# Convolution steps spread evenly over the weight gradient phases, up to just ahead of the output phase

## The chip, the cores and the metric

One core of a Trainium2 chip runs the whole program. The metric is the time of one execution on the device in microseconds (us). The kernel before takes 2009.09 us, the median of three runs (2007.18 to 2009.27).

## The reference

The program is the forward and backward pass of a block that adds two branches: a long convolution (a shift filter of four taps, a product with v, a convolution of length 2048 by FFT, a gate), and a gated MLP. Cut to its core:

```python
def reference(A_q, A_k, A_v, A_shift_k, A_ssm_k, A_ssm_D, B_W_gate, B_W_up, B_W_down, B_x, grad_out):
    # x = A_q;  xn = layernorm(x)                      S, D, F = 2048, 1024, 3584
    # out = x + A(xn, k, v, shift_k, ssm_k, ssm_D) + B(xn, W_gate, W_up, W_down)
    # A: kv = shift(k) * v;  y = irfft(rfft(kv) * rfft(ssm_k)) + kv * D;  result xn * y
    # B: h = relu(xn W_gate) * (xn W_up);  result h W_down
    _out, _vjp = jax.vjp(_f, A_q, A_k, A_v, A_shift_k, A_ssm_k, A_ssm_D, B_W_gate, B_W_up, B_W_down)
    return (_out, *_vjp(grad_out))
```

## The kernel before

The MLP runs in phases: *hidden* (gate, up and their gradients), *down gradient* (`grad_down`), *input gradient* (`grad_in`, the gradients of the gate and up weights), then the *output phase* and the gradient of x. The first three are generators that yield after every eight matmuls of 512 columns, a slot with a declared length of 1730 ns. The convolution is a generator too, of 408 steps in eight groups of channels. A small loop weaves them: every slot pays its length times a *pace* into an account, and when the account is open, steps are taken and charged.

```python
    def mlp():
        yield 0.9, b.hidden(first, goT, B_W_gate, B_W_up, B_W_down, g, xn_d, h_d, ug_d)
        yield 1.3, b.grad_down(g, h_d, out_9)
        yield 1.3, b.grad_in(xn_d, ug_d, out_7, out_8)

    a_steps, left = a.steps(), A_START
    if True:
        for pace, phase in mlp():
            for ns in phase:
                left -= ns * pace
                while a_steps is not None and left <= 0:
                    d = next(a_steps, None)
                    if d is None:
                        a.close()
                        a_steps = None
                        b.open_right(B_W_down)
                    else:
                        left += d
```

When the convolution is done its buffers are released, and W_down is loaded in their place for the output phase. Two kinds of step:

```python
    def fwd1(self, src, ns, add_D=None):      # first stage: pairs of 64-row matmuls, one cast B<-ps a step
        ...
    def fwd2(self, Bf, F, ns):                # second stage, for the spectra H, G and K
        for k0 in range(0, NB1, 8):
            ps = self.ps.tile([P, 8, P], F32, name="ps2", tag="aps")      # a pool of two tiles
            for j in range(8):
                self.mm(ps[:, j, :], self.FW[:, k0 + j].rearrange("p a k -> p (a k)"), Bf[:, k0 + j, :])
            kh, kl = k0 // 16, k0 % 16
            rows = slice(64 * kh, 64 * kh + 64)
            self.act(F[rows, 0, kl:kl + 8, :], ps[0:64])
            self.act(F[rows, 1, kl:kl + 8, :], ps[64:128])
            yield ns
    # ... pauses for VectorE stand between stages, such as: yield 12000, yield 5000
```

## Time and profile before

| | us |
|---|---|
| time, median of 3 | 2009.1 |
| hidden phase, to the first matmul of the down gradient | 723.2 |
| weight phases: from there to the first matmul of the output phase (1412.5) | 689.3 |
| output phase | 201.5 |
| gradient of x | 395.4 |

The casts of one spectrum on ScalarE, in the order line, engine, operation, output and input, form, count, busy time and mean ns of one, idle time before and its releasers:

```profile
L69 ACT CAST H<-ps 64x1024 bf16<-64x1024 f32 x64 | 64.4, 1006 | 5.0 <-PE ps L65 3.8
```

A `fwd2` step costs TensorE eight matmuls of 128 columns, 0.45 us, but ScalarE two casts, 2.0 us. Beside that ScalarE empties one accumulation of the MLP in every second slot, in 0.586 us.

### The profile page before, as it was taken

What the parts mean: (1) busy time and instruction counts of PE and PEld (TensorE: products, weight loads), DVE (VectorE), ACT (ScalarE), POOL (GpSimd) and SP (SyncE); (2) the same over time, 40 slices, a digit from 0 to 9 for tenths busy, and PEclk for the clock granted to TensorE, in tenths of its full rate; (3) what the DMA queues carried; (4) which work ended last, traced back from release to release, by engine and by line L of the source; (5) the groups of instructions that cost most, each with busy time, mean ns of one, the idle gap of its engine ahead of it and who ended that gap; (6) DMA issues with size and microseconds to landing.
All of it is one profiled execution on the core that took longest, in us unless ns stands there. A gap on an engine that the chain in (4) does not pass through costs nothing.

```text
span 2009.4 us, 27247 instructions
## 1 busy us (share of the span) xinstructions
PE 1944.6 (97%) x11022; PEld 916.2 (46%) x11022; DVE 996.6 (50%) x1460; ACT 694.6 (35%) x912; POOL 16.3 (1%) x36
## 2 busy tenths in 40 slices
PE   3999999999999999999999999999999999999998
PEld 1445445444444444444454444444444444444443
DVE  5769678677677756666585650000112222233332
ACT  6455456456447428384564741111000000000000
POOL 2000000000000000000000000000000000000000
PEclk8999999999999999999999999999999999999999
DMA  9864675975674674444655259422999545544551
GB/s 269 220 162 124 157 201 150 217 189 134 156 197 125 189 210 119 130 135 133 191 159 139 81 171 300 163 93 76 213 268 226 148 115 122 127 116 121 125 127 42
DMA packets 614895, 318.32 MB, mean 158 GB/s; under 512 B 449896, under 2 KB 584048, under 8 KB 614768
## 3 DMA queue, kind: packets, MB, share of 16 engines
q1 hardware_dynamic: 613488, 312.38, 59.3%
q0 software_dynamic: 1280, 4.20, 0.6%
q8 instruction: 86, 1.41, 0.3%
q14 instruction: 41, 0.34, 0.0%
HBM read 141.36 MB, written 95.44 MB: 118 GB/s over the span
## 4 chain that ended last, share of the span: by engine, by line
PE 47%; ACT 2%; DMA 1%; SPq 1%; issue 0%; DVE 0%; DVEq 0%
PE ps_x L822 19%; PE ps_w L705 17%; PE ps_o L789 8%; PE ps L65 1%; DMA hT<-h_d 1%; ACT G L69 1%; SPq L781 0%; ACT H L69 0%; ACT K L69 0%; ACT wi L743 0%; ACT B L69 0%; SPq L758 0%; PE pst L280 0%; DVE gx L837 0%; DVE gm L834 0%
## 5 line engine op out<-in xcount | busy, mean ns | idle before, releaser
L705 PE MATMUL ps_w<-ugs,xn_nat 128*128 128x512 bf16 x1792 | 400.2, 379 | 1.1 <-DMA xn_nat<-xn_d 1.0
L595 PEld LDWEIGHTS <-xnT 128*128 128x128 bf16 x1792 | 169.7, 99 | 215.8 <-issue 23.2
L705 PEld LDWEIGHTS <-xn_nat 128*128 128x128 bf16 x1792 | 170.9, 98 | 204.2 <-issue 8.2
L595 PE MATMUL ps_g<-wg,xnT 128*128 128x512 bf16 x896 | 213.6, 387 | 15.4 <-DVE xnT L621 11.4
L705 PE MATMUL ps_d<-g_nat,hs 128*128 128x512 bf16 x896 | 208.6, 381 | 3.6 <-DMA hs<-h_d 3.6
L595 PE MATMUL ps_h<-wdT,goT 128*128 128x512 bf16 x896 | 207.4, 379 | 0.0
L595 PE MATMUL ps_u<-wu,xnT 128*128 128x512 bf16 x896 | 207.3, 379 | 0.0
L789 PE MATMUL ps_o<-wd,hT 128*128 128x512 bf16 x896 | 195.8, 381 | 5.9 <-DMA hT<-h_d 5.9
L822 PE MATMUL ps_x<-wgT,ggT 128*128 128x512 bf16 x896 | 198.6, 379 | 0.0
L822 PE MATMUL ps_x<-wuT,guT 128*128 128x512 bf16 x896 | 198.6, 379 | 0.0
L791 DVE TENSOR_TENSOR o<-ps_o,ya 128x512 bf16<-128x512 f32 x32 | 21.6, 687 | 277.4 <-PE ps_o L789 277.3
L743 ACT CAST wi<-ps_w 128x512 bf16<-128x512 f32 x112 | 65.6, 586 | 233.4 <-PE ps_w L705 230.7
L789 PEld LDWEIGHTS <-hT 128*128 128x128 bf16 x896 | 87.9, 98 | 113.6 <-DMA hT<-h_d 7.4
L824 DVE CUSTOM_DVE_ANT_0 gx<-ps_x,gy 128x512 f32<-128x512 f32 x32 | 22.1, 692 | 229.9 <-PE ps_x L822 229.9
L822 PEld LDWEIGHTS <-ggT 128*128 128x128 bf16 x896 | 87.7, 98 | 105.7
L822 PEld LDWEIGHTS <-guT 128*128 128x128 bf16 x896 | 87.7, 98 | 105.7
L664 ACT CAST gh<-ps_h 128x512 bf16<-128x512 f32 x112 | 65.5, 586 | 191.9 <-PE ps_h L595 120.8
L705 PEld LDWEIGHTS <-hs 128*128 128x128 bf16 x896 | 83.1, 98 | 100.6 <-issue 9.7
L595 PEld LDWEIGHTS <-goT 128*128 128x128 bf16 x896 | 84.1, 98 | 97.8 <-issue 6.1
L291 DVE STREAM_TRANSPOSE flp<-B 128x1024 f32<-128x1024 f32 x48 | 90.2, 1935 | 47.8 <-ACT B L69 47.6
L69 ACT CAST C<-ps 128x1024 bf16<-128x1024 f32 x96 | 96.7, 1016 | 48.4 <-PE ps L65 48.4
L652 DVE SCALAR_TENSOR_TENSOR ru<-ru,ps_u 128x512 bf16<-128x512 bf16 x112 | 76.2, 681 | 64.4 <-PE ps_u L595 52.2
(156 smaller groups left out, 1714.5 us busy)
## 6 DMA issues: line engine op xcount, KB each, us to landing
ug_d<-ru SPq DMA_DIRECT2D x112, 256.0 KB, 3.5
ugs<-ug_d SPq DMA_DIRECT2D x112, 256.0 KB, 4.4
wg<-in_B_W_gate_dram SPq DMA_DIRECT2D x56, 256.0 KB, 4.7
wu<-in_B_W_up_dram SPq DMA_DIRECT2D x56, 256.0 KB, 3.2
h_d<-ht SPq DMA_DIRECT2D x112, 128.0 KB, 2.2
hs<-h_d SPq DMA_DIRECT2D x56, 256.0 KB, 4.6
out_dram<-wi SPq DMA_DIRECT2D x56, 256.0 KB, 2.1
gt<-in_grad_out_dram SPq DMA_DIRECT2D x32, 256.0 KB, 4.0
```

The costliest lines, as they stand in the source:

```text
L65: self.nc.tensor.matmul(out, lhsT=lhsT, rhs=rhs, start=start, stop=stop)
L69: self.nc.scalar.copy(out=out, in_=in_)
L291: self.nc.vector.transpose(out=df[:, c0:c0 + 32, :], in_=sf[:, c0:c0 + 32, :])
L595: self.nc.tensor.matmul(ps[:], lhsT=xT[:, kt * P:(kt + 1) * P], rhs=w(kt), start=(kt == 0), stop=(kt == self.DT - 1))
L652: nc.vector.scalar_tensor_tensor(out=ru[s][:, 1, :], in0=ru[s][:, 0, :], scalar=0.0, in1=ps[:], op0=ALU.is_gt, op1=ALU.mult)
L664: nc.scalar.copy(out=gh[:], in_=ps[:])
L705: self.nc.tensor.matmul(ps[:], lhsT=lhsT(st), rhs=rhs(st), start=(st == 0), stop=(st == self.ST - 1))
L743: nc.scalar.copy(out=wo[:, d, :], in_=ps[:])
L789: nc.tensor.matmul(ps[:], lhsT=hT[:, kt, :], rhs=self.wd[:, kt, oc], start=(kt == 0), stop=(kt == self.FT - 1))
L791: nc.vector.tensor_tensor(out=o0[:, oc], in0=ps[:], in1=ya[:, oc], op=ALU.add)
L822: nc.tensor.matmul(ps[:], lhsT=T[:, kt, :], rhs=W[:, kt, oc], start=(i == 0), stop=(i == n - 1))
L824: V.tensor_tensor_reduce(out=gx[:, oc], in0=ps[:], in1=gy[:, oc], scale=1.0, scalar=0.0, op0=ALU.add, op1=ALU.add, accum_out=m[:, ob:ob + 1])
```

## The change

Its intent is to use the whole of the two weight phases for the convolution instead of the first two thirds, and to end it just early enough for the loads of the output phase.

```diff
-        yield 1.3, b.grad_down(g, h_d, out_9)
-        yield 1.3, b.grad_in(xn_d, ug_d, out_7, out_8)
+        yield 1.0, b.grad_down(g, h_d, out_9)
+        yield 1.0, b.grad_in(xn_d, ug_d, out_7, out_8)
```

## The prediction

> **What bounds the kernel now.** I read the page first, then busy time per stage, then what TensorE waited for in the stages that the change touches, then the order of time in one run of steps, and last the end of the convolution against the start of the output phase. From the page, busy share per engine, and two rows of the 40 slices:
>
> ```profile
> PE 1944.6 (97%) x11022; PEld 916.2 (46%) x11022; DVE 996.6 (50%) x1460; ACT 694.6 (35%) x912; POOL 16.3 (1%) x36
> ...
> PE   3999999999999999999999999999999999999998
> ...
> PEclk8999999999999999999999999999999999999999
> ```
>
> TensorE works in every slice but the first, at nearly full clock. All that can be saved is 2009.4 - 1944.6 = 64.8 us of idle time, wherever it lies. Busy time by stage (the columns are the stretch, its length, busy time of PE, PEld, DVE, ACT and POOL, the granted clock, DMA share, GB/s):
>
> ```profile
> 735.00:976.00 241.00, 236.57 (x1621) 116.55 (x1620) 148.43 (x152) 137.08 (x165) 0.81 (x2) 1.00 0.49 137
> 976.00:1205.00 229.00, 224.92 (x1525) 109.90 (x1524) 146.71 (x152) 136.18 (x162) 0.41 (x1) 1.00 0.51 148
> 1205.00:1412.30 207.30, 207.30 (x965) 94.03 (x965) 2.54 (x4) 35.16 (x60) 0.00 (x0) 1.00 0.49 155
> ```
>
> The first two rows are the weight gradients with convolution steps between them, the third is the rest of the weight gradients after the convolution has ended. In the third PE is never idle; in the first two it is idle for 4.4 + 4.1 = 8.5 us. TensorE's idle time by group in 735 to 1205 us shows whose it is:
>
> ```profile
> L705 PE MATMUL ps_w<-ugs,xn_nat 128*128 128x512 bf16 x832 | 192.8, 379 | 1.1 <-DMA xn_nat<-xn_d 1.0
> L65 PE MATMUL ps<-flp,FW 128*128 128x128 bf16 x384 | 28.8, 219 | 4.3 <-ACT K L69 1.5 <-ACT G L69 1.0 <-DVE flp L291 1.0
> ...
> L65 PE MATMUL ps<-kvt,R 64*128 64x512 bf16 x32 | 6.1, 383 | 2.3 <-ACT B L69 1.3 <-ACT H L69 0.9
> ```
>
> Three more convolution groups have 0.8 us, so the convolution's steps account for 4.3 + 2.3 + 0.8 = 7.4 us, and 1.1 us is a load. 7.4 us is all that a better spread of steps can win here, 0.37% of the time. How it arises is seen in time order in one group (TensorE and ScalarE lines only):
>
> ```profile
> 1107.67 1.06 PE L65 MATMUL ps<-flp,FW 128*128 128x128 bf16 x16
> 1108.31 3.06 ACT L69 CAST H<-ps 64x1024 bf16<-64x1024 f32 x3 [1.10 <-PE ps L65]
> 1108.56 1.89 PE L705 MATMUL ps_w<-ugs,xn_nat 128*128 128x512 bf16 x8
> 1110.39 0.61 PE L65 MATMUL ps<-flp,FW 128*128 128x128 bf16 x8
> ...
> 1112.94 0.61 PE L65 MATMUL ps<-flp,FW 128*128 128x128 bf16 x8 [0.21 <-ACT H L69]
> ```
>
> Sixteen matmuls of 128 columns are two steps in one slot. They fill both of the convolution's two PSUM tiles at once; ScalarE empties a tile in two casts of about 1.01 us, so it falls behind and TensorE waits 0.2 us for the tile two steps later. Small stalls of this kind, and nothing larger, are the target. For comparison, what TensorE waited for from 60 to 715 us, the hidden phase, whose pace is 0.9:
>
> ```profile
> PE ps_g L595 <- DVE ru L652: 3.9, 2, 2.2
> PE ps_g L595 <- DVE xnT L621: 1.8, 1, 1.8
> PE ps L65 <- DVE flp L291: 1.3, 1, 1.3
> PE pst L280 <- ACT ghn L69: 0.2, 1, 0.2
> ```
>
> At pace 0.9, some four channel groups of the convolution cost TensorE only 1.3 + 0.2 = 1.5 us of waits, and none of it is for a PSUM tile of the forward transforms.
>
> **What the Trainium skill says.** "TensorE: Matmul & The Clock Gate", Back-to-back issue gap, gives an isolated spacing of N/2.4 + 2.5 ns at full clock, 215.8 ns for 512 columns, and a lower 131 ns for pipelined streams. The trace agrees with the first and not with the second: the pure stretch has 960 matmuls in 207.31 us, 215.9 ns each. So the stretch without the convolution cannot be sped up by what is taken from it. The same page, What's actually happening, says that TensorE falls back to half clock after an idle window of about 3.4 us. The trace agrees: after the 3.62 us wait for hs at 728.76 us, the next 24 matmuls took 6.65 us, 277 ns each, 1.5 us more than at full clock. The stalls of 0.2 to 1.0 us that I count here are too short for that and the clock of their stages reads 1.00, so removing them brings their own length and no clock. "Perfetto Trace Analysis", Identifying Performance Opportunities, says that the same gap repeating on the engine that should be saturated can mean too few buffers; the 0.2 to 0.5 us gaps at the two PSUM tiles fit this.
>
> **The change part by part.** It removes and adds no instruction. TensorE has 22046 rows in the instruction order of either kernel, and the first difference is in the first matmuls of the down gradient; only positions move. The pacing follows from the code. The convolution has 408 steps, 51 for each of 8 groups, with declared lengths that sum to 952,000 ns; with the start offset of 55,000 it needs 1,007,000. The hidden phase offers 336 slots of 1730 ns x 0.9 = 523,152. The remaining 483,848 take 483,848 / (1730 x 1.3), the 216th of the 336 slots of the weight gradients before, and 483,848 / 1730, the 280th, after. The trace confirms the first: 120 slots x 8 matmuls are the 960 of the pure stretch. Walking the list through both paces, 29 slots of the weight phases take two steps now and 1 will.
>
> *Saved.* With one step per slot, a forward-transform step needs TensorE for 8 x 55 ns plus 8 x 216 ns, 2.17 us per slot, and ScalarE for 2 x 1.01 us plus half an eviction of 0.586 us, 2.31 us. ScalarE thus still falls behind by 0.14 us per step, but for four steps, 0.6 us in all; its two PSUM tiles give a step two slots, 4.3 us, from write to reuse, while the casts need about 3. So these waits should go almost entirely. I take the hidden phase's 1.5 us as what is left: 7.4 - 1.5 = 5.9 us saved.
>
> *Moved on DVE and ACT.* Both get the same work over 64 more slots. At 62 to 64% and 57 to 59% busy in these stages they are no bound before, and less so after.
>
> *Moved at the end.* The convolution's end moves from slot 216 to 280, leaving 56 slots, 448 matmuls x 215.9 ns = 96.7 us, to load what the output phase needs. I count nothing for it (see the rivals). The sum is 2009.1 - 5.9 = 2003.2; a few tenths for new collisions make it 2003.5.
>
> **Rivals.** *ScalarE stays the limit of the forward transforms.* The 0.14 us per step speaks for it. Against it are the two tiles of slack. If half of the 7.4 us stayed, the time would be 2005.5.
>
> *The output phase waits for W_down.* Its weights (four loads of 1.8 MB) can only go where the convolution's tiles lay. Before, the convolution ended at 1205.3 and the first two and the last of the loads were issued at
>
> ```profile
> 1232.88 1.00 SPq L753 DMA_DIRECT2D wd<-in_B_W_down_dram  x2
> ...
> 1253.25 0.37 SPq L753 DMA_DIRECT2D wd<-in_B_W_down_dram  x1
> ```
>
> each landing after 12.5 us. In the changed order the fourth load again stands behind the loads of a slab of ug, here the last slab, which waits for the buffers of the slab two before it. Those come free at about 1412.3 - 2 x 16 slots x 1.727 = 1357 us (before the saving). Issue at some 1362 and landing at some 1375 leave 37 us. Also three transposes of hT, 12.5 us of the queue, come before the next slab's loads, when that slab has a half left of the one in use. If I am wrong, TensorE waits and then runs at half clock for a while: 2012 to 2025. I give this one chance in twenty.
>
> *The start of the input gradient loses its filling.* At 976 us TensorE consumes xn_nat as fast as it is loaded. Before, 14 first-stage matmuls of the convolution stood among them and it waited 1.0 us. After, inverse-transform steps of a quarter of the length stand there, though the order shows the scheduler interleaving up to three accumulations to stretch each loaded tile. This could cost 1 to 3 us: 2004.5 to 2006.5.
>
> *More than the stalls is won.* Nothing in the trace supports it: full clock and back-to-back matmuls elsewhere.
>
> **Range and chances.** The three runs before span 2.1 us, and the saving is bounded by 7.4. The best case is about 2001; half the saving eaten by one of the mild rivals gives 2006, and nothing won 2009. I take 2000.5 to 2008.5 for eight in ten. Faster by over 2% would need 40 us, more than every idle microsecond after the start-up: 0.01. Slower by over 2% would need the output phase to stand for 40 us: 0.02. Within 2%: 0.97.
>
> **What would show it.** Right: the pure stretch of ps_w shrinks from 960 matmuls to about 448 and ends in the output phase without a wait for wd; TensorE's waits for ACT H, G, K and B in the weight phases fall from about 5 us to under 1.5; its busy time stays near 1945; the stall of hs at 728 us and the 5.9 us for hT in the output phase stay as they are. Wrong: ps_o waiting for wd, a wait for xn_nat of several us with a granted clock under 1.00 after it, or waits for casts that persist though steps come singly, which would mean that ScalarE's rate and not the doubling of steps makes them.

## The result, and the profile after

The changed kernel takes 2000.6 us (median of 4 runs, 1996.99 to 2004.62), against 2009.18 for the kernel before in the same rounds. Ratios are the mean time of one kernel's runs over that of the other's of the same rounds, so not quite the ratio of the medians quoted. Here the ratio is 0.9956 (95% interval 0.9931 to 0.998). So some 8.7 us were won where 5.6 were predicted, and with the ratio applied to the 2009.1 us of the prediction the result lies just under its range.

What TensorE waited for in the weight phases (who, on what, us in total, times, longest). Of the kernel before, up to the convolution's end, the waits for ScalarE's casts:

```profile
PE ps L65 <- ACT K L69: 1.5, 5, 0.5
PE ps L65 <- ACT B L69: 1.3, 2, 0.8
PE ps L65 <- ACT H L69: 1.3, 5, 0.3
...
PE ps L65 <- ACT G L69: 1.0, 4, 0.3
```

Of the changed kernel, up to the convolution's end:

```profile
PE ps_d L705 <- DMA hs<-h_d: 3.2, 1, 3.2
PE ps L65 <- DVE flp L291: 1.0, 1, 1.0
PE ps_w L705 <- DMA xn_nat<-xn_d: 0.8, 1, 0.8
...
PE ps L65 <- ACT H L69: 0.6, 2, 0.3
```

The waits for ScalarE's casts of H, G, K and B, 5.1 us in all before, are 0.8 us (0.6 for H, and 0.2 for B). The waits for hs and for xn_nat are much as they were. A run of `fwd2` steps in time order on TensorE (start, length, instruction):

```profile
908.64 0.61 PE L65 MATMUL ps<-flp,FW 128*128 128x128 bf16 x8
909.09 1.89 PE L705 MATMUL ps_d<-g_nat,hs 128*128 128x512 bf16 x8
910.81 0.61 PE L65 MATMUL ps<-flp,FW 128*128 128x128 bf16 x8
```

One step and one slot alternate, 2.17 us from one step to the next, with nothing lost. And the end of the convolution:

```profile
1307.58 96.87 PE L705 MATMUL ps_w<-ugs,xn_nat 128*128 128x512 bf16 x439
1404.29 72.68 PE L789 MATMUL ps_o<-wd,hT 128*128 128x512 bf16 x329
```

The pure stretch has shrunk from 207.3 to 96.7 us as computed, and ps_o follows it without a gap; the last load of W_down was issued at 1352.77 us. This trace has lost 208 of 11022 matmul records, one in 53, so that 439 stand for 448. Each lost record leaves a small gap in the view of waits, marked as issue; those lines are left out above. For the same reason the busy time of TensorE in this trace (1930.2 us) can't be compared with that of before.

The gain is in the weight phases. Their length, from the first matmul of the down gradient to the first of the output phase, is 680.7 us against 689.3 (8.6 less), the output phase is 1.7 us shorter and the rest 0.3 longer. Yet by the idle column the waits of the convolution's steps fell by 5.3 us only. What makes up the rest was the question of the experiments, along with what the pace really acts on.

**Stalls read from start times.** In the prediction's lines of the kernel before, sixteen FW matmuls start at 1107.67 and the next slot at 1108.56; sixteen at 56 ns are 0.89 us, nothing lost. The slot's eight matmuls take 8 x 216 = 1.73 us, so the next step could start at 1110.29; it starts at 1110.39, 0.10 us late, and the view marks no wait. The slot after it starts at 1110.84 (a line that the prediction leaves out), so its successor could start at 1112.57; it starts at 1112.94, 0.37 us late, and the view shows 0.21. The view counts idle time from the *end* of a matmul's record, 379 ns after its start for 512 columns and 219 ns for 128, while the successor can start after 216 or 56. So 163 ns of every stall are covered by the record, and a shorter stall isn't seen at all. I therefore summed, for all neighbours on TensorE, the distance of their starts beyond the usual shortest one for that pair of kinds. For the steps of the forward stages and of the per-channel inverse in the weight phases this gives 12.4 us before, of which the idle column shows 7.3, and 3.2 us after, of which it shows 2.0. The fall is 9.2 us, 5.3 of it visible and 3.9 hidden. By kind, second-stage (FW) steps fell from 7.5 to 1.3, first-stage (R) steps from 3.9 to 1.5, and the per-channel inverse (RB) steps from 1.0 to 0.4. The exact figures hang on the shortest distances chosen: a second count from the same traces gives 12.1 us before and 3.0 after, with the same 7.3 and 2.0 in the idle column.

**Something is given back.** A first-stage step costs more alone than in twos, as TensorE's lines of the kernel before show:

```profile
862.24 0.60 PE L65 MATMUL ps<-hT,R 64*128 64x512 bf16 x4
862.78 0.82 PE L705 MATMUL ps_d<-g_nat,hs 128*128 128x512 bf16 x3
...
867.83 1.90 PE L705 MATMUL ps_d<-g_nat,hs 128*128 128x512 bf16 x8
869.67 0.39 PE L65 MATMUL ps<-gt,R 64*128 64x512 bf16 x2
869.99 1.90 PE L705 MATMUL ps_d<-g_nat,hs 128*128 128x512 bf16 x8
```

A single step: the slot before takes 1.84 us instead of 1.73, and the two 64-row matmuls, which run side by side, 0.32 instead of 0.22. That is 0.21 us for going to 64 rows and back. Two steps together take 0.54 us, one such fee instead of two. The Trainium skill ("TensorEngine Tiling (Array Packing)", Key Properties) says that changing the tiling mode drains TensorE; these lines agree. The instruction order has seven such doubles in the weight phases before and one after, so 6 x 0.21 = 1.3 us are lost again. Net, 9.2 - 1.3 = 7.9 us; the three traces of the changed kernel have weight phases of 680.7, 682.3 and 680.0 us, 8.3 us less than before in the mean, some 1 us of which is a shorter wait for hs and the half clock after it.

### The profile page after: what moved, and what is told of

It is laid out like the page before. It is cut to its first block, busy times and chain, and to the rows that moved or that the text cites. A ratio compares the mean times of both kernels' runs of the same rounds, so it can differ in the third digit from the quotient of the medians.

```text
span 1999.4 us, 27038 instructions
## 1 busy us (share of the span) xinstructions
PE 1930.2 (97%) x10814; PEld 915.0 (46%) x11022; DVE 996.9 (50%) x1460; ACT 695.5 (35%) x912; POOL 16.3 (1%) x36
## 4 chain that ended last, share of the span: by engine, by line
PE 58%; SPq 1%; DMA 1%; issue 0%; ACT 0%; DVE 0%; DVEq 0%
PE ps_x L822 19%; PE ps_w L705 19%; PE ps_o L789 8%; PE ps_d L705 8%; PE ps L65 4%; SPq L781 1%; DMA hT<-h_d 0%; PE pst L280 0%; DMA xn_nat<-xn_d 0%; SPq L758 0%; ACT H L69 0%; SPq L699 0%; SPq L775 0%; ACT B L69 0%; SPq L773 0%
## 5 line engine op out<-in xcount | busy, mean ns | idle before, releaser
L705 PE MATMUL ps_d<-g_nat,hs 128*128 128x512 bf16 x869 | 204.4, 382 | 4.7 <-DMA hs<-h_d 3.2
L291 DVE STREAM_TRANSPOSE flp<-C 128x1024 f32<-128x1024 f32 x48 | 89.7, 1928 | 51.4 <-ACT C L69 51.4
L69 ACT CAST B<-ps 128x1024 bf16<-128x1024 f32 x96 | 96.5, 1019 | 45.8 <-PE ps L65 45.7
```

Of the source, the lines that this page charges most:

```text
L69: self.nc.scalar.copy(out=out, in_=in_)
L291: self.nc.vector.transpose(out=df[:, c0:c0 + 32, :], in_=sf[:, c0:c0 + 32, :])
L705: self.nc.tensor.matmul(ps[:], lhsT=lhsT(st), rhs=rhs(st), start=(st == 0), stop=(st == self.ST - 1))
```

## The experiments

All kernels ran on the chip with their own runs of the kernel before in the same rounds. The theory when they began (theory 1) was the prediction's: slots with *two* steps make the stalls. The rivals were the place of the end, and a difference between runs.

**1. One step per slot at pace 1.3** (cap13).

```diff
                     else:
                         left += d
+                        if n > 0:        # n: 0 hidden, 1 and 2 the weight phases
+                            break
```

> Pace 1.3 kept in both weight gradient phases, but at most one convolution step per slot: no slot takes two steps (29 did), and the convolution still ends at slot 216. Theory 1 (the gain is the removal of double steps, whose stalls the idle column shows only in part, because a matmul's record lasts 379 or 219 ns while its successor can start after 216 or 56): 2000 to 2002 us, as the changed kernel, with the pure stretch of ps_w still 960 matmuls. Theory 2 (the gain comes from where the convolution ends, that is from the loads and the output phase): 2008 to 2010, as before. Theory 3 (only the visible idle time was won, and the rest of the 8.8 us is a difference between runs): 2003 to 2004.

Measured: 2006.74 us, ratio 0.9994 (0.9981 to 1.0008), the same as before. The stalls of FW steps did fall, from 7.5 to 2.1 us. But the longest wait of TensorE in the weight phases is now for VectorE's transposes (1.2 us before):

```profile
PE ps L65 <- DVE flp L291: 6.5, 5, 1.4
```

With one step a slot at this pace the account stays overdrawn after a run, and the pauses that were to give VectorE time pay off the debt instead. Walking the list through the loop, two slots instead of three lie between the last step that fills C and the first RB step. The inverse steps then come before VectorE's transposes are done; RB steps lose 6.6 us instead of 1.0. So this run doesn't decide between the theories: this cap spared ScalarE at pace 1.3, and VectorE's pauses paid for it.

**2. Twos on purpose at pace 1.0** (pair10).

```diff
+            for slot, ns in enumerate(phase):
                 left -= ns * pace
+                if n > 0 and slot % 2 == 0:
+                    continue
```

> Pace 1.0, but steps are handed out only in every second slot of the weight gradient phases, so that they come in twos: 84 slots with two steps, end at slot 280 as in the changed kernel. Theory 1, at about 0.3 us for a double step (some 8.8 us for 28): up to 25 us over the changed kernel if every double costs the same, at least 8 us if only those in the forward transforms do: 2009 to 2026. Theory 2 (place of the end): 2000 to 2002.

Measured: 1997.02 us, ratio 0.9943 (0.993 to 0.9956). Theory 1 falls. The instruction order shows 20 of 48 FW steps directly behind another step of the convolution (16 of them behind another FW step), where the kernel before has nine, and yet TensorE waits for ScalarE hardly at all in the weight phases:

```profile
PE ps L65 <- ACT H L69: 0.9, 3, 0.3
```

and 0.2 us for G.
Two PSUM tiles take up two steps at once, and two slots follow in which ScalarE catches up. What counts is how many steps come per slot over a run, not that two come together. This is the *density theory*: at 1.3 steps per slot ScalarE needs 1.3 x 2.02 + 0.29 = 2.9 us a slot for its casts, and TensorE 1.73 + 1.3 x 0.45 = 2.3; at one step per slot it is 2.3 against 2.2, and four steps in a row are over before the lag fills the two tiles.

**3. The changed kernel again** (even10).

> The changed kernel once more, with more rounds, to see how much of the gain beyond the predicted 5.6 us is a difference between runs. Theory 1: 8 to 9 us under before (2000 to 2001). Theory 3: nearer 6 us under before (2003).

Measured: 1999.6 us, ratio 0.9957 (0.9944 to 0.9969). It is no difference between runs.

**4. Pace 0.87** (late087), the two paces of the change set to 0.87.

> Pace 0.87 in the weight gradient phases: no double steps, but the convolution ends at slot 322, 14 slots or 24 us before the output phase. If the stalls were all gone at 1.0 there is nothing more to win. Theory 1 and the rival that W_down comes late: the four loads were issued 27 to 48 us after the convolution's end before and take 12.5 us, so ps_o waits some 15 to 37 us for wd: 2015 to 2040. If the place of the end does not matter: 2000 to 2002.

Measured: 2013.23 us, ratio 1.002 (1.0002 to 1.0038). The weight phases take 683.4 us, so nothing more is won there; the wait for xn_nat at the start of the input gradient, one of the prediction's rivals, is 2.4 us here instead of 0.8. The output phase takes 211.3 us instead of 201.5, for TensorE waits in it:

```profile
PE ps_o L789 <- DMA hT<-h_d: 10.7, 6, 3.1
PE ps_o L789 <- DMA wd<-in_B_W_down_dram: 3.4, 2, 3.0
```

The loads of W_down were issued from 1397.71 to 1406.83 us, and the output phase began at 1405.6. The direct wait is 3.4 us, less than the 15 to 37 expected: this time the scheduler put the loads 17 to 26 us behind the convolution's end, not 27 to 48, and a load is needed only when its part of the sum comes. But the transposes of the gate and up weights, which share the queue with hT's, are pushed back too: the first was issued 10.8 us after the start of the output phase, before it was 3.1. That this made hT late is likely, but was not tried by itself. "Just ahead of the output phase" thus has an edge between slot 280 and 322 of 336.

**5. Uneven, with the same end** (uneven): `grad_down` 1.3, `grad_in` 0.8, the end at slot 280.

> Pace 1.3 in the down gradient, 0.8 in the input gradient: the convolution ends at slot 280 as in the changed kernel, but about half of its steps keep the old density. Density theory (what stalls TensorE is the rate at which steps follow one another in a run: each forward step gives ScalarE 2.0 us of casts, so at 1.3 steps per slot ScalarE falls behind and at 1.0 it does not): the down gradient keeps its stalls, about half of the gain is lost, 2003 to 2006. End theory (only the place of the end counts): 1999 to 2001.

Measured: 2002.92 us, ratio 0.997 (0.9957 to 0.9983): a part of the gain is lost, as the density theory has it, though the end lies where it does in the changed kernel. The interval overlaps that of the changed kernel (0.9944 to 0.9969), but the weight phases of the trace, 686.0 us, lie between 689.3 and the 680.0 to 682.3 of the changed kernel. The FW stalls by start times are 5.1 us (before 7.5, changed 1.3), and the waits for ScalarE are back (those for G and H, with 0.6 us for K besides):

```profile
PE ps L65 <- ACT G L69: 0.8, 3, 0.3
PE ps L65 <- ACT H L69: 0.8, 3, 0.3
```

This trace has all its matmuls. The place of the end alone is thus not what won the time.

**6. Pace 1.0 in the hidden phase too** (hidden10).

> Pace 1.0 in all three phases: steps as dense as in the changed kernel in the weight gradients, but the convolution ends at slot 247, about half way between before (216) and the changed kernel (280). Density theory: 1999 to 2002, and the waits for casts in the weight gradients stay as low as in the changed kernel. End theory: about half of the gain, 2004 to 2005.

Measured: 2011.58 us, ratio 1.0011 (0.9999 to 1.0023). Neither theory said this. The weight phases, with fewer steps in them, take 664.2 us and their FW steps hardly stall at all (0.1 us), as the density theory says. But the hidden phase took 746.9 us, 23.7 more than before, while the weight phases are only 16.8 us shorter than the changed kernel's 681.0 (the mean of its three traces). More than half of the 23.7 us is convolution work that has moved from one phase into the other; the loss is what is left over. Among the waits new in the hidden phase are

```profile
PE ps_u L595 <- ACT gh L664: 2.7, 1, 2.7
...
PE pst L280 <- ACT ghn L69: 2.4, 1, 2.4
...
PE ps L65 <- ACT H L69: 2.4, 6, 0.7
```

By start times the FW steps of this phase lose 5.2 us, where the traces with pace 0.9 and unchanged casts on ScalarE show at most 0.2.

In that phase ScalarE also applies the ReLU and empties the gradient sums, two casts in three slots, so it has less room for convolution steps. This reading rests on the waits; experiments 8 and 9 below, with fewer casts, shorten the hidden phase too. I had judged pace 1.0 by the weight phases alone.

**7. Half of the `fwd2` casts on VectorE, pace 1.3** (dve13).

```diff
-            self.act(F[rows, 1, kl:kl + 8, :], ps[64:128])
+            self.vcopy(F[rows, 1, kl:kl + 8, :], ps[64:128])
```

> Pace 1.3 as before, but the second of the two casts of each forward step goes to VectorE, so ScalarE has 1.0 us instead of 2.0 us a step. Density theory: the waits of forward steps for casts (7.5 us of stalls before) fall to under 2.5 us though 29 slots still take two steps, and the time is 2001 to 2005, unless VectorE[...] brings waits of its own. End theory: 2008 to 2010.

Measured: 2037.51 us, ratio 1.014 (1.0124 to 1.0157), a miss. TensorE now waits for VectorE:

```profile
PE ps L65 <- DVE K L77: 15.8, 8, 2.9
PE ps L65 <- DVE H L77: 6.2, 7, 1.7
```

These sums are over the whole time up to the output phase: the hidden phase took 737.1 us instead of 723.2, the weight phases 701.7 instead of 689.3. VectorE was busy 62 to 64% of the weight phases before and is busy 70 to 75% with the casts, each of which takes it 1.22 us where ScalarE needs 1.01. What stands ahead of a cast counts too. From 1037.63 us on VectorE multiplies H and G without a pause; of the K tiles that TensorE fills from 1038.09 and 1040.26, VectorE's half is cast only after these products:

```profile
1040.26 0.61 PE L65 MATMUL ps<-flp,FW 128*128 128x128 bf16 x8
...
1045.15 2.78 DVE L73 TENSOR_TENSOR GKV<-t 64x1024 bf16<-64x1024 bf16 x4
1047.96 2.37 DVE L77 CAST K<-ps 64x1024 bf16<-64x1024 f32 x2
...
1049.24 0.61 PE L65 MATMUL ps<-flp,FW 128*128 128x128 bf16 x8 [1.24 <-DVE K L77]
```

The run says that the release of the PSUM tiles is what TensorE waits for, and nothing on ScalarE's rate. That needed a kernel in which ScalarE's work shrinks and nobody's grows.

**8. and 9. One cast instead of two, at pace 1.3 and at 1.0** (onecast13, onecast10; the result is wrong on purpose, with spectra in the wrong places and a relative error of 1.2).

```diff
-            self.act(F[rows, 0, kl:kl + 8, :], ps[0:64])
-            self.act(F[rows, 1, kl:kl + 8, :], ps[64:128])
+            self.act(F[:, kh, kl:kl + 8, :], ps[:])
```

> Pace 1.3 as before, the convolution's end at slot 216 as before, 29 double steps as before, but each step of the forward second stage leaves PSUM in one cast of 128 partitions (about 1.02 us) instead of two of 64 (2.02 us). The spectra then lie in the wrong places: the result is wrong on purpose, the work of every other engine is the same. Density theory (ScalarE's 2.0 us of casts per forward step against the slots' rate): the stalls of forward steps (7.5 us of 128-column steps and 3 us of the first-stage steps among them before) fall to some 2 us; weight phases about 681 us instead of 689; 1999 to 2002. If ScalarE is not what holds TensorE: 2008 to 2010.

> The same single casts (wrong result on purpose) at pace 1.0. Density theory: with ScalarE relieved there is little left for the pace to win, so this is within 2 us of the single casts at pace 1.3, where the two paces differ by 8 to 9 us with the double casts. If the pace works by something else than ScalarE: 6 us or more under the single casts at 1.3.

Measured: 1994.09 us at pace 1.3, ratio 0.993 (0.9918 to 0.9942), and 1993.63 us at pace 1.0, ratio 0.993 (0.9917 to 0.9943). With ScalarE relieved the two paces are equal to within the intervals (some 2.5 us each way), where they differ by 8.7 us with the double casts. At 1.3, with the same pacing, doubles and end as before, the weight phases take 680.0 us, the length of the changed kernel, and FW steps lose 1.5 us. A double there (the sixteen matmuls) and what follows:

```profile
881.25 1.06 PE L65 MATMUL ps<-flp,FW 128*128 128x128 bf16 x16
882.36 3.40 PE L704 MATMUL ps_d<-g_nat,hs 128*128 128x512 bf16 x15
885.59 0.61 PE L65 MATMUL ps<-flp,FW 128*128 128x128 bf16 x8
```

No wait follows the double (one of the records of the slots is missing here). The times are lower than expected because the hidden phase gained as well: 715.5 and 716.9 us instead of 719.5 to 723.6 in the traces with that phase untouched. This pair settles the cause: the pace acts on the time through ScalarE's casts. It doesn't tell the rate of the casts from the time that the casts of one tile take, since both are halved. That the stalls go at pace 1.0 with both casts in place speaks for the rate.

**10. The changed kernel beside them** (even10b).

> The changed kernel again, on the same chip as the single-cast kernels; with luck with all its matmuls in the trace (208 of them are missing in the one at hand). Hidden-stall reading (an idle gap is counted only after the end of a matmul's record, 379 or 219 ns after its start, though the next could start after 216 or 56): visible idle time in the weight phases after the wait for hs is 2 to 4 us against 8.5 before, 5 to 6 us less, while the stretch itself is 7 to 9 us shorter. If the idle column showed all: the stretch is 5 to 6 us shorter. Time 1999 to 2001.

Measured: 2000.62 us, ratio 0.9958 (0.9946 to 0.997). The trace again lacked 208 matmuls. The weight phases take 680.0 us, 9.3 less than before. By start times the three kinds of steps lose 2.9 us instead of 12.4, and the idle column shows 1.8 of it instead of 7.3. The stretch shrank by more than the visible 5.5 us, as the hidden-stall reading says.

**11. Twos again beside it** (pair10b).

> Steps in twos at pace 1.0 again, beside the changed kernel on the same chip: twos were 2 to 3 us faster in the first call, with intervals that just overlap. If a change from 128-row to 64-row matmuls and back costs about 0.2 us, as the start times suggest, the 15 changes fewer at the R steps save 3 us: 1996 to 1998. If it was a difference between runs: 1999 to 2001.

Measured: 1995.9 us, ratio 0.9946 (0.9933 to 0.9958). Twice the twos were 2 to 3 us ahead of the changed kernel of the same call, with intervals that overlap. The saved changes of tiling mode (15 x 0.21 = 3.2 us by the order and the start times) would be of this size, but that they are the cause is not shown. The traces don't bear it out: the weight phases with twos take 679.9 and 680.9 us, against 681.0 in the mean of the changed kernel's three traces, and one of the two has a longer wait for xn_nat (2.0 us). It is the fastest correct kernel, by 0.1%.

**12. Twos, and the weights' transposes in the output phase in halves** (pair_spread): in place of a transpose of 256 rows in each of the first 8 passes, one of 128 rows in each of the 16.

> Steps in twos at pace 1.0 (1997 us in the last call), and with it the sixteen transposes of the gate and up weights in the output phase one half as large in each of its 16 passes, instead of 8 whole ones in the first 8. If the waits of ps_o for hT (5 to 8 us of stalls in every run so far) come from the queue being held 7 to 8 us by each of these transposes, they go: 1990 to 1994. If they come from elsewhere: 1996 to 1998.

Measured: 2001.6 us, ratio 0.9961 (0.9949 to 0.9973), no gain over the twos alone (0.9943 and 0.9946). The wait of ps_o for hT stayed: 6.7 us in three times, where the kernel before had 5.9. The scheduler issued two halves one behind the other between the transposes of hT, for 8 to 10 us, so the queue was held as long as ever. Whether halves that are kept apart would help is left open.

## Why the prediction was right or wrong

*Where the gain lies* was right: in the weight phases, in the convolution's waits for PSUM tiles that ScalarE empties. The single casts of experiments 8 and 9 show it.

*Nothing lost at the end* was right: W_down landed in time, the pure stretch shrank to 448 matmuls, and the wait at the start of the input gradient stayed small (0.8 us, 1.0 before). The rival had its chance at pace 0.87.

*The size was wrong, and the step that failed is "7.4 us is all that a better spread of steps can win here", with "removing them brings their own length".* The 7.4 us are an idle column. It starts to count when a matmul's modelled record ends, 163 ns after the next could have started. By start times the same steps lost 12.4 us. The term "7.4 - 1.5 = 5.9 us saved" measures 12.4 - 3.2 = 9.2, less 1.3 for more changes between 128 and 64 rows, which the prediction didn't count. What the idle column itself showed fell by 5.3 us, close to the 5.9 predicted. The two figures that would have corrected it stood in the prediction's own lines, 379 ns for a record and 215.9 ns from start to start. The Trainium skill also warns of it: "Perfetto Trace Analysis", Tensor Engine Instruction, says that the end of a TensorE record is an estimate from the instruction's size, and "TensorE: Matmul & The Clock Gate", Single matmul latency, gives (398 + N)/2.4 ns, 379 for 512 columns and 219 for 128, exactly the records here.

*The mechanism was half wrong.* The prediction saw the cause in slots that take two steps. Experiment 2 has more of them and no such stalls. It is the density over a run, and the two sums of the prediction's own *Saved* paragraph (2.31 against 2.17 us) were the right ones. The pace was the right lever all the same, since it lowers the density; that it was chosen for the sake of the doubles and worked is in part luck.

*What remains open* is small: some 0.4 us between the mean of the weight phases' gain (8.3 us) and the gain in time, less than the 4 us by which the hidden phase of the same instructions differs from trace to trace. Open is also why the twos of experiments 2 and 11 gain another 2 to 3 us.

## What to carry to other kernels

Where side work is woven into a bound engine's stream, set its pace by the engine that drains the side work, and by phase: steps per slot times the casts of a step must fit beside the casts that the phase has already, and the pauses must stay long enough for the engine behind it. Judge stalls of TensorE by the distance of starts, not by the idle column alone: many small gaps are worth more than they show, here by about two thirds. When two changes of pace differ, take away the suspected engine's work (even with a wrong result) and see whether the paces become equal.

## What the Trainium skill lacked or had wrong

- "Perfetto Trace Analysis", Identifying Performance Opportunities, tells the reader to look for gaps between slices. For TensorE it should add that a gap appears only beyond the latency: 163 ns of each are covered here (379 - 216, 219 - 56), and 12.4 us of stalls showed as 7.3.
- "TensorE: Matmul & The Clock Gate", Back-to-back issue gap, gives 131 ns as the sustained spacing at 512 columns. Here 960 such matmuls took 207.31 us, 215.9 ns each; the page's formula for the isolated gap (215.8) is what a stream keeps to, as other sections of the same page have it (215.7 measured), so that the page disagrees with itself.
- "TensorEngine Tiling (Array Packing)", Key Properties, says that changing the tiling mode drains TensorE and gives no cost. Here a pair of 64-row matmuls between 128-row ones cost 0.21 us more than its own length.
- "Perfetto Trace Analysis", Optimizing Scalar/DVE Operations, treats the choice between ScalarE and VectorE for an operation as one of speed and saturation, and says only in general that engines which aren't saturated can cause bubbles on others. A warning is missing there that a cast which frees PSUM can stand behind long products on VectorE: with VectorE 70 to 75% busy in the weight phases the move cost 28 us (2037.5 against 2009.0), and VectorE's half of a K tile filled from 1038.09 us was not cast before 1047.96.
